# A fused attention and token-mixing block: its first operations written out engine by engine, phi loaded compact, x laid out by tiles

## The chip, the cores and the metric

One core of a Trainium2 chip runs the kernel. The metric is the device time of one execution in microseconds; lower is better. The engines are PE (TensorE, matrix products; its weight loads are listed as PEld), DVE (VectorE), ACT (ScalarE), POOL (GpSimd) and SP (SyncE, which issues most DMAs). Each runs its own list of instructions in order, and they wait for one another through semaphores.

## What is computed

x has 2048 rows (tokens) of 512 numbers. First an attention with a learned feature map, per head (32 heads of 16), then an MLP across the tokens:

```
xn  = layernorm(x)
q, k, v = split(xn @ wqkv)                                  # 32 heads of 16 each
phi(y)  = concat(softmax(y @ w_phi), softmax(-(y @ w_phi))) # per head
o   = phi(q) (phi(k)^T v) / (phi(q) (phi(k)^T 1) + 1e-6)
h   = x + o @ wo
y   = w2^T gelu(w1^T layernorm(layernorm(h)) + b1) + b2     # w1, w2 act on the token axis
out = h + y
```

Everything is in 32-bit floats. To keep the precision with the faster kind of product, the kernel splits each operand in a high part (a copy rounded by the operand type, `F32R`) and a low part (the difference), and takes three products: high·high, high·low and low·high.

## The kernel before

The tokens are cut into 16 tiles of 128 rows (`NT`), the 512 features into 4 blocks of 128 (`KD`). The kernel has three stages: attention with the K, V and Q projections (up to about 135 us of the span), then the attention's output and the first part of the MLP, then the two MLP products. The change touches the beginning of the first stage.

**Weights.** `wT` is the transposed `wqkv`, in 12 row blocks of 128 x 512: blocks 0 to 3 belong to Q, 4 to 7 to K, 8 to 11 to V. Each block c is loaded (`load_w`), freed of its mean (`center(c)`: the mean is taken off the weights so that the layernorm's mean need not be taken off x; even blocks on VectorE in three instructions, odd ones on ScalarE in two), brought to the orientation that the projections need (`fold(c)`, four matmuls: with the block-diagonal phi matrix `ph` for Q and K blocks, so that w_phi is folded into the weights, and as a plain transpose by `ident` for V blocks), and then split (`split_w`: the high part on ScalarE, the low part on VectorE). `fold` writes to a PSUM tile of `ps_q` or `ps_v`, with two buffers each.

**Tiles of x.** `load_x(t)` brings the transposed tile, `split_x(t)` splits it: the high part on ScalarE, the low part on GpSimd. `load_h(t)` brings the same rows untransposed, and `stats_x(t)` takes their variance: two ScalarE passes with accumulation, a small VectorE instruction and a power on GpSimd, which gives the scale `r1`.

**Projections.** `proj` is 12 matmuls of 512 columns: for each of 4 blocks the three products of `mm3`. `k_logits(t)` projects tile t on K and makes the logits with four VectorE instructions (`logit_ops`: a maximum, a minimum, two differences), then ScalarE takes the exponential (`exps`). `k_norm(t)` takes sums and reciprocals on VectorE and multiplies on GpSimd, which also adds up `zacc`. `v_proj(t)` projects on V, and ScalarE scales it with `r1`. `kv(t)` takes 32 small matmuls into one accumulator.

**Order.** The framework's planner sorts instructions of all engines by a model of their times. Inside a `manual_schedule` block the listed engines get the instructions of the block in the order of the program text; instructions from outside the block can still be placed between them. In the kernel before, the block at lines 267 to 301 lists VectorE and ScalarE, so the order of TensorE and GpSimd is the planner's. It covers the centering, folding and splitting of all weights, `split_x(0)`, `split_x(1)` and two `stats_x`. Then a loop over t = 0 to 14 (lines 330 to 349) has for each tile: the loads of tile t + 2, `k_logits(t)`, a `v_proj` except for t in `V_NOT` (5, 8 and 11), `kv` of a tile three back, `k_norm(t - 1)`, `split_x` and `stats_x` of t + 2, and, for t in `Q_AT`, one Q projection with its logits, exponential and sums. This loop is ordered by the planner on all engines. A later written block does the rest of V and goes on with Q.

**Buffers.** `xraw` has two buffers, `xh` three, `pk` six (`len(V_NOT) + 3`); `ps_k` and `ps_v` two each. `ps_k` also holds the target of nine warm-up matmuls that keep TensorE working while the first loads come in.

**Queue.** All loads go out on SP's queue, in the order of lines 215 to 233: two weight blocks, `ph` (256 KB, in rows of 512 bytes), two more weight blocks, `xraw` of tile 0, and so on. The transposed x is a matrix of 512 x 2048, so the rows of one tile's load are 512 bytes long.

Of the kernel before, what the change touches and what calls it, by code (L numbers as in the profile page):

```python
# [9 lines left out]
F32 = mybir.dt.float32  # L10
# [5 lines left out]
ET = mybir.EngineType  # L16

P = 128
# [6 lines left out]
Q_AT = (3, 5, 8, 9, 11, 13)  # L25
V_NOT = (5, 8, 11)
SUMS = 8
# [5 lines left out]
@with_exitstack  # L33
def block_kernel(ctx: ExitStack, tc: tile.TileContext, x, xT, wT, phibd, wo, w1, b1, w2, b2,
                 kvmask, ident_in, out):
# [60 lines left out]
    def load_x(t):  # L96
        raw = kk.tile([P, KD, P], F32, name="xraw")
        nc.sync.dma_start(raw, xT[:, t * P:(t + 1) * P].rearrange("(k p) s -> p k s", p=P))
        return raw
# [65 lines left out]
    def heads(e):  # L165
        return e.rearrange("p g (a d) -> p (g a) d", d=DH)

    def k_logits(t):
        PK[t] = kk.tile([P, NG, P], F32, name="pk", bufs=len(V_NOT) + 3)
        run(logit_ops(proj(t, wkh, wkl, ps_k, "pk_ps"), PK[t], False))  # L170
        exps(t, PK[t])
# [32 lines left out]

    with tc.tile_pool(name="prep", bufs=1) as prep:
        ph = prep.tile([P, 4, P], F32, name="ph")
        WR = {}
# [29 lines left out]

        def center(c):

            mu = prep.tile([P, 1], F32, name="mu", bufs=3)  # L240
            if c % 2 == 0:
                nc.vector.reduce_sum(mu, WR[c], axis=AX.X)
                nc.vector.tensor_scalar_mul(mu, mu, -1.0 / D)
                nc.vector.tensor_scalar(WR[c], WR[c], mu, None, op0=ALU.add)
            else:
                junk = prep.tile([P, D], F32, name="junk")
                nc.scalar.activation(junk, WR[c], AF.Copy, scale=-1.0 / D, accum_out=mu)
                nc.scalar.activation(WR[c], WR[c], AF.Identity, bias=mu)
# [9 lines left out]

        def split_w(c):
            hi, lo = HL[c // 4]  # L260
            cols = slice((c % 4) * P, (c % 4 + 1) * P)
            split(hi[:, :, cols], lo[:, :, cols], FO[c], nc.vector)

        warm = ps_k.tile([P, P], F32, name="pk_ps", tag="pk_ps")
        for _ in range(WARM):
            nc.tensor.matmul(warm, ones, ones, start=True, stop=True)
        with tc.manual_schedule(engines={ET.DVE, ET.Activation}):
            center(4)
            center(5)
            fold(4, ps_q, "pu")  # L270
            center(6)
            fold(5, ps_q, "pu")
            center(7)
            split_w(4)
            split_w(5)
            split_x(0, xr[0])
            fold(6, ps_v, "pv")
            split_w(6)
            fold(7, ps_v, "pv")
            split_w(7)  # L280
            center(8)
            center(9)
            fold(8, ps_q, "pu")
            fold(9, ps_q, "pu")
            center(10)
            center(11)
            split_w(8)
            split_w(9)
            fold(10, ps_q, "pu")
            fold(11, ps_q, "pu")  # L290
            split_x(1, xr[1])
            split_w(10)
            split_w(11)
            stats_x(0)
            stats_x(1)
            for c in range(4):
                center(c)
            for c in range(4):
                fold(c, ps_q, "pu")
                split_w(c)  # L300

# [446 lines left out]
def _layout(A_x, A_wqkv, A_w_phi, A_wo, B_w1, B_b1, B_w2, B_b2):  # L748
    x = np.asarray(A_x)[0]
    wqkv = np.asarray(A_wqkv)  # L750
    phi = np.asarray(A_w_phi)
    bd = np.zeros((4, P, P), np.float32)
    for h in range(H):
        b, o = divmod(h, P // DH)
        bd[b, o * DH:(o + 1) * DH, o * DH:(o + 1) * DH] = phi[h]
    mask = np.zeros((P, 64), np.float32)
    for a in range(P // DH):
# [6 lines left out]
        "x": x,  # L764
        "xT": x.T,
        "wT": wqkv.T,
        "phibd": bd,
        "wo": wo,
# [25 lines left out]
```

## Time and profile before

| | us |
|---|---|
| median of three timed runs | 545.8 (544.52, 545.8, 545.85) |
| the profiled execution's own time | 544.96 |
| its span | 543.2 |
| TensorE busy | 528.6 (97% of the span) |
| VectorE busy | 393.8 (73%) |
| ScalarE busy | 256.5 (47%) |
| GpSimd busy | 234.2 (43%) |

The span runs from the first to the last instruction of the execution that the profiler recorded; the time of an execution holds 1.76 us more here. A row of a timeline gives the start in us from the span's start, the duration, the engine, the line of the kernel, the operation, what is written and what is read, the shape, and in brackets how long the engine had been idle and what ended that. A row of the chain of waits gives start, length, engine, tile, line and count. In a row of grouped instructions the numbers after the bar are the busy time in us and the mean ns of one, then the idle time ahead of them. Matmuls are pipelined: one is listed with its latency, while the next one starts before it ends, so the cost of a matmul in a dense row is the distance of two starts.

### The profile page before, as it was taken

The page shows a single profiled execution, that of the slowest core. Times are in us where ns is not written, and L with a number is a line of the kernel's source. Part 1 is how long each engine was busy: PE and PEld are TensorE (multiplying, and loading weights), DVE is VectorE, ACT ScalarE, POOL GpSimd, SP SyncE. Part 2 cuts the span into 40 slices and gives each one's busy share as a digit, 9 for nine tenths or more (in the row PEclk, how much of TensorE's full clock was granted, in tenths as well). Part 3 has the DMA queues.
Part 4 walks back from the last instruction along what each step waited for, and adds up shares of the span by engine and source line. Part 5 has one row for each costly group of instructions (what it writes and reads, how often), then busy time and mean ns, then how long its engine had stood idle before and what let it go on. Part 6 is the DMA issues. An engine that isn't in the chain of part 4 may idle for free.

```text
span 543.2 us, 9896 instructions
## 1 busy us (share of the span) xinstructions
PE 528.6 (97%) x3872; PEld 449.7 (83%) x3872; DVE 393.8 (73%) x726; ACT 256.5 (47%) x402; POOL 234.2 (43%) x183
## 2 busy tenths in 40 slices
PE   7999999999999999999999999999999999999996
PEld 6687787877777777777787788888899999999996
DVE  4783999975689998996546862223947878878874
ACT  6599935334344555445546533224643433433330
POOL 1369799798978888997342200000001011101110
PEclk9999999999999999999999999999999999999998
DMA  8434402004121223333234543333103655535631
GB/s 307 128 117 118 134 22 58 2 1 138 38 60 59 81 76 117 118 117 118 98 118 154 173 140 97 97 97 97 39 14 107 152 138 134 136 133 121 156 73 45
DMA packets 52014, 56.06 MB, mean 103 GB/s; under 512 B 3840, under 2 KB 41600, under 8 KB 51968
## 3 DMA queue, kind: packets, MB, share of 16 engines
q1 hardware_dynamic: 49808, 51.64, 30.2%
q0 software_dynamic: 2016, 3.67, 4.9%
q8 instruction: 30, 0.49, 0.4%
q14 instruction: 16, 0.13, 0.1%
q10 hardware_dynamic: 144, 0.13, 0.1%
HBM read 47.04 MB, written 8.39 MB: 102 GB/s over the span
## 4 chain that ended last, share of the span: by engine, by line
PE 87%; DVE 7%; ACT 3%; DMA 2%; issue 1%; SPq 0%; DVEq 0%; ACTq 0%
PE py L687 25%; PE pu L61 11%; PE pu L63 11%; PE pu L62 10%; PE pk_ps L61 3%; PE pk_ps L62 3%; PE pk_ps L63 3%; PE po L61 3%; PE pv L61 3%; PE pv L62 3%; PE pv L63 3%; PE po L62 2%; PE po L63 2%; PE tn L468 2%; PE kvp L194 2%; PE tn L486 1%
## 5 line engine op out<-in xcount | busy, mean ns | idle before, releaser
L57 DVE TENSOR_TENSOR wlo<-wraw,whi 128x512 fp32r<-128x512 f32 (+1 forms) x84 | 99.6, 1197 | 72.4 <-ACT whi L56 72.3
L56 ACT ACTIVATE whi<-wraw 128x512 fp32r<-128x512 f32 (+1 forms) x84 | 81.9, 986 | 128.9 <-PE py L687 73.8
L725 POOL DMA_DIRECT2D out<-ot x14 | 12.4, 998 | 205.0 <-DVE ot L723 205.0
L687 PE MATMUL py<-uf,whi 128*128 128x256 f32 x560 | 96.2, 283 | 0.0
L61 PE MATMUL pu<-hs,whi 128*128 128x512 f32 x224 | 87.6, 394 | 0.6 <-ACT eq L140 0.6
L63 PE MATMUL pu<-hs,wlo 128*128 128x512 f32 x224 | 86.4, 392 | 1.1 <-DVE wlo L57 1.1
L62 PE MATMUL pu<-hs,whi 128*128 128x512 f32 x224 | 87.3, 390 | 0.0
L687 PEld LDWEIGHTS py<-uf,whi 128*128 128x128 f32 x560 | 83.3, 192 | 0.0
L687 PE MATMUL py<-uf,wlo 128*128 128x256 f32 x280 | 69.9, 283 | 0.0
L63 PEld LDWEIGHTS pu<-hs,wlo 128*128 128x128 f32 x224 | 41.7, 188 | 11.2 <-DVE wlo L57 2.7
L61 PEld LDWEIGHTS pu<-hs,whi 128*128 128x128 f32 x224 | 42.1, 188 | 9.5 <-ACT eq L140 1.1
L687 PEld LDWEIGHTS py<-uf,wlo 128*128 128x128 f32 x280 | 49.7, 192 | 0.0
L62 PEld LDWEIGHTS pu<-hs,whi 128*128 128x128 f32 x224 | 42.1, 188 | 8.4
L470 ACT ACTIVATE pht<-tn 128x512 f32<-128x512 f32 x32 | 17.4, 596 | 50.5 <-PE tn L468 50.5
L376 POOL TENSOR_TENSOR ez<-eq,zB 128x1024 f32<-128x1024 f32 x16 | 38.3, 2399 | 0.7 <-ACT zB L430 0.7
L687 PE MATMUL py<-un,whi 128*128 128x256 f32 x224 | 38.4, 283 | 0.0
L182 POOL TENSOR_TENSOR pk<-pk,sk 128x1024 f32<-128x1024 f32 x16 | 31.1, 1941 | 9.3 <-ACT xs L56 3.0
L687 PEld LDWEIGHTS py<-un,whi 128*128 128x128 f32 x224 | 33.2, 192 | 0.1
L394 POOL TENSOR_TENSOR eq<-eq,w 128x1024 f32<-128x1024 f32 x16 | 31.0, 1940 | 4.4 <-DVE w L391 4.4
L186 POOL TENSOR_TENSOR zacc<-zacc,pk 128x1024 f32<-128x1024 f32 x13 | 31.2, 2403 | 0.5
L57 POOL TENSOR_TENSOR xs<-xraw,xs 128x512 fp32r<-128x512 f32 x16 | 20.5, 1290 | 24.2 <-ACT xs L56 24.2
L57 POOL TENSOR_TENSOR hs<-hn,hs 128x512 fp32r<-128x512 f32 x16 | 20.6, 1289 | 21.2 <-ACT hs L56 21.2
(152 smaller groups left out, 1152.8 us busy)
## 6 DMA issues: line engine op xcount, KB each, us to landing
wraw<-in_w SPq DMA_DIRECT2D x112, 256.0 KB, 2.9
xraw<-in_xT SPq DMA_DIRECT2D x16, 256.0 KB, 3.1
xh<-in_x SPq DMA_DIRECT2D x16, 256.0 KB, 2.7
h<-in_x SPq DMA_DIRECT2D x16, 256.0 KB, 2.9
out<-h SPq DMA_DIRECT2D x16, 256.0 KB, 2.3
out<-ot POOLq DMA_DIRECT2D x14, 256.0 KB, 4.7
wraw<-in_wT SPq DMA_DIRECT2D x12, 256.0 KB, 5.1
wo<-in_wo SPq DMA_DIRECT2D x4, 256.0 KB, 4.5
```

The costliest lines, as they stand in the source:

```text
L56: nc.scalar.activation(hi, src, AF.Copy)
L57: lo_engine.tensor_sub(lo, src, hi)
L61: nc.tensor.matmul(o, ah, bh, start=first, stop=False)
L62: nc.tensor.matmul(o, ah, bl, start=False, stop=False)
L63: nc.tensor.matmul(o, al, bh, start=False, stop=last)
L182: nc.gpsimd.tensor_mul(heads(PK[t]), heads(PK[t]), sk.unsqueeze(2).to_broadcast([P, 2 * H, DH]))
L186: nc.gpsimd.tensor_add(zacc, zacc, PK[t])
L376: nc.gpsimd.tensor_mul(EZ[t], EQ[t], zB)
L394: nc.gpsimd.tensor_mul(heads(EQ[t]), heads(EQ[t]), W[t].rearrange("p g c h -> p (g c h)").unsqueeze(2).to_broadcast([P, 2 * H, DH]))
L470: nc.scalar.activation(PHT[t][:, half * 4:half * 4 + 4, :], ptr[:, half], AF.Copy)
L687: nc.tensor.matmul(o, a[x], b[:, y], start=start and i == 0, stop=stop and i == 2, skip_group_check=True)
L725: nc.gpsimd.dma_start(out[(t + i) * P:(t + i + 1) * P, :], flat(ot[:, i]), accum_op=ALU.add)
```

## The change

The first operations of all four computing engines are put into one `manual_schedule` block, and their order is written out.

- **phi.** Instead of the block-diagonal matrix of 4 x 128 x 128 the kernel gets `phic`, 128 x 72: the 64 columns of w_phi and an 8-column mask. It is loaded on ScalarE's queue, and one GpSimd multiplication with two broadcast operands makes `ph` from it.
- **x.** `xT` is laid out by tiles, so that each partition reads one row of 2 KB. `xraw` gets three buffers.
- **Loads.** SP's order is: w4 to w7, x0, x1, ident, w8 to w11, x2, h0, h1, x3, w0 to w3, h2, x4, h3, then the small ones.
- **Splitting weights.** `split_w` becomes `hi_w` (ScalarE, or VectorE for blocks 4 and 5) and `lo_w` (VectorE). Block 10 is centered on ScalarE instead of VectorE.
- **Order.** K is projected for tiles 0, 1 and 2 before the first V projection, with the V blocks' transposes between K1 and K2; then V0, K3, the folds of blocks 0 and 1, and V1. K0 is taken by parts (`by_part`): all four high·high products, then low-x·high, then high·low. Logits, exponentials, statistics and `k_norm(0)`, `k_norm(1)` stand at written places.
- **Loop.** It now begins at t = 3, with K from t = 4 and V from tile 2 at t = 4; `V_NOT` is (0, 1, 8).

```diff
-V_NOT = (5, 8, 11)
+V_NOT = (0, 1, 8)
...
-        raw = kk.tile([P, KD, P], F32, name="xraw")
-        nc.sync.dma_start(raw, xT[:, t * P:(t + 1) * P].rearrange("(k p) s -> p k s", p=P))
+        raw = kk.tile([P, KD, P], F32, name="xraw", bufs=3)
+        nc.sync.dma_start(raw, xT[t])
...
-    def proj(t, wh, wl, pool, name):
+    def proj(t, wh, wl, pool, name, by_part=False):
         o = pool.tile([P, D], F32, name=name, tag=name)
+        if by_part:
+            for i, (a, w) in enumerate(((0, wh), (1, wh), (0, wl))):
+                for kt in range(KD):
+                    nc.tensor.matmul(o, X[t][:, a, kt, :], w[:, kt, :], start=i == 0 and kt == 0,
+                                     stop=i == 2 and kt == KD - 1)
+            return o
...
-        load_w(4)
-        load_w(5)
-        nc.sync.dma_start(ph, phibd.rearrange("c p f -> p c f"))
-        load_w(6)
-        load_w(7)
-        xr = {0: load_x(0)}
-        load_w(8)
+        nc.scalar.dma_start(pc, phic)
+        for c in range(4, 8):
+            load_w(c)
+        xr = {0: load_x(0), 1: load_x(1)}
         nc.sync.dma_start(ident, ident_in)
-        load_w(9)
+        for c in range(8, 12):
+            load_w(c)
+        xr[2] = load_x(2)
         load_h(0)
-        load_w(10)
-        load_w(11)
-        xr[1] = load_x(1)
         load_h(1)
+        xr[3] = load_x(3)
         for c in range(4):
             load_w(c)
+        load_h(2)
+        xr[4] = load_x(4)
+        load_h(3)
...
-        def center(c):
+        def center(c, vector):
...
-            if c % 2 == 0:
+            if vector:
...
-        def split_w(c):
-            hi, lo = HL[c // 4]
-            cols = slice((c % 4) * P, (c % 4 + 1) * P)
-            split(hi[:, :, cols], lo[:, :, cols], FO[c], nc.vector)
+        def parts(c):
+            return [w[:, :, c % 4 * P:(c % 4 + 1) * P] for w in HL[c // 4]]
+
+        def hi_w(c, vector=False):
+            if vector:
+                nc.vector.tensor_copy(parts(c)[0], FO[c])
+            else:
+                nc.scalar.activation(parts(c)[0], FO[c], AF.Copy)
+
+        def lo_w(c):
+            hi, lo = parts(c)
+            nc.vector.tensor_sub(lo, FO[c], hi)
...
-        with tc.manual_schedule(engines={ET.DVE, ET.Activation}):
+        with tc.manual_schedule(engines={ET.PE, ET.DVE, ET.Activation, ET.Pool}):
+
+            nc.gpsimd.tensor_mul(ph.rearrange("p c (a f) -> p c a f", f=DH),
+                                 pc[:, 0:64].rearrange("p (c f) -> p c f", f=DH).unsqueeze(2).to_broadcast([P, 4, 8, DH]),
+                                 pc[:, 64:72].unsqueeze(1).unsqueeze(3).to_broadcast([P, 4, 8, DH]))
+            center(4, True)
+            center(5, False)
             fold(4, ps_q, "pu")
+            center(6, True)
             fold(5, ps_q, "pu")
+            center(7, False)
+            fold(6, ps_v, "pv")
+            fold(7, ps_v, "pv")
+            hi_w(4, True)
+            hi_w(5, True)
+            hi_w(6)
             split_x(0, xr[0])
+            hi_w(7)
+            for c in range(4, 8):
+                lo_w(c)
             split_x(1, xr[1])
+            k0 = proj(0, wkh, wkl, ps_k, "pk_ps", True)
+            center(8, True)
+            for c in range(9, 12):
+                center(c, False)
+            k1 = proj(1, wkh, wkl, ps_k, "pk_ps")
+            for c in range(8, 12):
+                fold(c, *((ps_q, "pu"), (ps_v, "pv"))[c // 10])
+            k_ops(0, k0)
+            split_x(2, xr[2])
+            k_ops(1, k1)
             stats_x(0)
+            k2 = proj(2, wkh, wkl, ps_k, "pk_ps")
+            for c in range(8, 12):
+                hi_w(c)
+            for c in range(8, 12):
+                lo_w(c)
+            exps(0, PK[0])
+            split_x(3, xr[3])
+            k_ops(2, k2)
+            v_proj(0)
             stats_x(1)
+            exps(1, PK[1])
+            k_norm(0)
+            k3 = proj(3, wkh, wkl, ps_k, "pk_ps")
+            center(0, True)
+            center(1, False)
+            split_x(4, xr[4])
+            k_ops(3, k3)
+            stats_x(2)
+            exps(2, PK[2])
+            fold(0, ps_q, "pu")
+            fold(1, ps_q, "pu")
+            hi_w(0)
+            hi_w(1)
+            lo_w(0)
+            lo_w(1)
+            v_proj(1)
+            k_norm(1)
+            center(2, True)
+            center(3, False)
+        stats_x(3)
+        exps(3, PK[3])
+        for c in range(2, 4):
+            fold(c, ps_q, "pu")
+            hi_w(c)
+            lo_w(c)
...
-    v = 0
-    for t in range(NT - 1):
+    v = 2
+    load_h(4)
+    stats_x(4)
+    for t in range(3, NT - 1):
         if t + 2 < NT:
             raw = load_x(t + 2)
             load_h(t + 2)
-        k_logits(t)
-        if t not in V_NOT:
+        if t > 3:
+            k_logits(t)
+        if t > 3 and t not in V_NOT:
             v_proj(v)
...
-        "xT": x.T,
+        "xT": x.reshape(NT, P, KD, P).transpose(0, 3, 2, 1),
...
-        "phibd": bd,
+        "phic": phic,
```

`k_ops(t, o)` is the first half of the old `k_logits`: it allocates `PK[t]` and makes the logits from the projected tile o.

More of the change, by code (lines that the diff above doesn't have):

```diff
@@ L33, in block_kernel @@
 @with_exitstack
-def block_kernel(ctx: ExitStack, tc: tile.TileContext, x, xT, wT, phibd, wo, w1, b1, w2, b2,
+def block_kernel(ctx: ExitStack, tc: tile.TileContext, x, xT, wT, phic, wo, w1, b1, w2, b2,
                  kvmask, ident_in, out):
@@ L166, in heads, with k_ops @@
         return e.rearrange("p g (a d) -> p (g a) d", d=DH)
+    def k_ops(t, o):
+        PK[t] = kk.tile([P, NG, P], F32, name="pk", bufs=len(V_NOT) + 3)
+        run(logit_ops(o, PK[t], False))
     def k_logits(t):
-        PK[t] = kk.tile([P, NG, P], F32, name="pk", bufs=len(V_NOT) + 3)
-        run(logit_ops(proj(t, wkh, wkl, ps_k, "pk_ps"), PK[t], False))
+        k_ops(t, proj(t, wkh, wkl, ps_k, "pk_ps"))
         exps(t, PK[t])
@@ L205, in block_kernel @@
     with tc.tile_pool(name="prep", bufs=1) as prep:
+        pc = prep.tile([P, 72], F32, name="pc")
         ph = prep.tile([P, 4, P], F32, name="ph")
@@ L266, in block_kernel @@
             nc.tensor.matmul(warm, ones, ones, start=True, stop=True)
-        with tc.manual_schedule(engines={ET.DVE, ET.Activation}):
-            center(4)
-            center(5)
+        with tc.manual_schedule(engines={ET.PE, ET.DVE, ET.Activation, ET.Pool}):
[4 more added lines that the diff above has]
+            center(5, False)
@@ L270, in block_kernel @@
             fold(4, ps_q, "pu")
-            center(6)
+            center(6, True)
             fold(5, ps_q, "pu")
-            center(7)
-            split_w(4)
-            split_w(5)
-            split_x(0, xr[0])
[L277 to L287, printed above, removed]
@@ L288, in block_kernel @@
-            split_w(9)
-            fold(10, ps_q, "pu")
-            fold(11, ps_q, "pu")
-            split_x(1, xr[1])
-            split_w(10)
-            split_w(11)
-            stats_x(0)
-            stats_x(1)
[L296 to L300, printed above, removed]
+            center(7, False)
+            fold(6, ps_v, "pv")
+            fold(7, ps_v, "pv")
+            hi_w(4, True)
@@ L751, in _layout @@
     phi = np.asarray(A_w_phi)
[L752 to L755, printed above, removed]
+    phic = np.concatenate([phi.reshape(4, P, DH).transpose(1, 0, 2).reshape(P, 64),
+                           np.kron(np.eye(8), np.ones((DH, 1)))], axis=1).astype(np.float32)
     mask = np.zeros((P, 64), np.float32)
```

## The prediction

> **What bounds the kernel now.** I read the page first, then busy time by stretches, then TensorE's waits.
>
> ```profile
> span 543.2 us, 9896 instructions
> PE 528.6 (97%) x3872; PEld 449.7 (83%) x3872; DVE 393.8 (73%) x726; ACT 256.5 (47%) x402; POOL 234.2 (43%) x183
> PE 87%; DVE 7%; ACT 3%; DMA 2%; issue 1%; SPq 0%; DVEq 0%; ACTq 0%
> ```
>
> TensorE is busy for 97% of the span and carries 87% of the chain that ended last. An edit ahead of the loops can only win TensorE time that is empty now. Stretches (length, then PE, PEld, DVE, ACT, POOL busy, clock, DMA share, GB/s):
>
> ```profile
> 0.00:5.19 5.19, 3.80 (x18) 3.64 (x19) 1.50 (x5) 2.42 (x4) 0.20 (x4) 1.00 0.65 200
> 5.19:24.14 18.95, 15.40 (x84) 12.10 (x85) 12.66 (x24) 10.89 (x23) 4.26 (x4) 1.00 0.71 243
> 24.14:60.00 35.86, 35.86 (x254) 28.83 (x255) 25.44 (x52) 34.54 (x79) 28.33 (x26) 1.00 0.42 123
> 60.00:120.00 60.00, 60.00 (x463) 47.60 (x463) 56.37 (x91) 28.66 (x41) 53.18 (x32) 1.00 0.12 34
> ```
>
> From 24.14 to 120 us TensorE has no gap at all, so what is won before 24.14 is kept as a shift, if that density is kept. Before 5.19 it runs only the warm-up. Between them, 84 matmuls take 18.95 us; these waits stand there (total us, times, longest), and the rows of the timeline and of the chain behind them give the prices:
>
> ```profile
> PE pk_ps L61 <- ACT wkh L56: 1.3, 1, 1.3
> PE pk_ps L61 <- ACT xs L56: 1.3, 1, 1.3
> PE pk_ps L62 <- DVE wkl L57: 0.3, 1, 0.3
> PE pu L254 <- DMA ph<-in_phibd: 0.3, 1, 0.3
> ```
> ```profile
> 5.19 2.02 PE L254 MATMUL pu<-ph,wraw 128*128 128x128 f32 x16 [0.33 <-DMA ph<-in_phibd]
> 11.44 0.49 PE L61 MATMUL pk_ps<-wkh,xs 128*128 128x512 f32 x1 [1.31 <-ACT wkh L56]
> 24.14 0.74 PE L61 MATMUL pv<-wvh,xs 128*128 128x512 f32 x2
> 29.98 0.39 PE L61 MATMUL pk_ps<-wkh,xs 128*128 128x512 f32 x1
> 33.38 0.39 PE L61 MATMUL pk_ps<-wkh,xs 128*128 128x512 f32 x1
> ```
> ```profile
> 15.09 0.45 PE pu L257 x4
> 33.77 0.89 PE pu L254 x8
> 38.31 0.58 PE kvp L194 x32
> ```
>
> From 29.98 to 33.38 lie 15 starts, so one 512-column matmul costs 0.227 us and a projection of twelve 2.72. A fold with phi costs 0.89, a fold by transpose 0.45. The 84 are four of each and three K projections: 3.56 + 1.80 + 8.16 = 13.5 us of work in 18.95. **5.4 us is to be had there**, plus what the first fold can start earlier.
>
> **The change, part by part.** *Loads.* The phi matrix of 256 KB, third in SP's queue, goes; a compact one of 37 KB goes out on ScalarE's queue, w4 to w7 follow one another, and x comes in 2 KB rows instead of 512-byte ones.
>
> ```profile
> 3.39 0.69 DVE L242 TENSOR_REDUCE mu<-wraw 128x1 f32<-128x512 f32 x1 [2.37 <-DMA wraw<-in_wT]
> 4.30 0.49 DVE L244 TENSOR_SCALAR wraw<-wraw,mu 128x512 f32<-128x512 f32 x1
> 5.93 0.69 DVE L242 TENSOR_REDUCE mu<-wraw 128x1 f32<-128x512 f32 x1 [1.15 <-DMA wraw<-in_wT]
> ```
> ```profile
> 4.02 0.63 ACT L247 ACTIVATE junk<-wraw 128x512 f32<-128x512 f32 x1 [2.00 <-DMA wraw<-in_wT]
> 4.78 0.72 ACT L248 ACTIVATE wraw<-wraw,mu 128x512 f32<-128x512 f32 x1
> 7.44 0.63 ACT L247 ACTIVATE junk<-wraw 128x512 f32<-128x512 f32 x1 [1.95 <-DMA wraw<-in_wT]
> ```
> ```profile
> 0.74 0.85 SPq L213 DMA_DIRECT2D wraw<-in_wT  x2
> ```
> ```profile
> 5.60:6.70 1.10, 1.10 (x12) 1.10 (x11) 0.74 (x2) 0.00 (x0) 0.00 (x0) 1.00 0.91 299
> 9.00:13.50 4.50, 2.85 (x14) 2.17 (x15) 3.79 (x8) 4.44 (x10) 1.27 (x1) 1.00 1.07 394
> ```
>
> The sums start when their tile lands: w4 3.39, w5 4.02, w6 5.93, w7 7.44. Spaced like w4 and w5 (0.63), or at 256 KB by 299 GB/s (0.88), w6 lands at 4.65 to 4.9 and w7 at 5.3 to 5.8. I take the former, as all rows are then long ones; worst is no change.
>
> The Trainium skill, "DMA: Bandwidth & Descriptors", section Specifications, gives line rate from 512 bytes up, so by it longer rows bring nothing. The trace speaks against it: 299 GB/s with 512-byte rows in flight, 394 without most of them. By the rule only phi's missing 0.9 us would count, w7 would land at about 6.6, and the gain would be some 0.4 us smaller.
>
> *Phi on GpSimd.* No row shows this multiply. The nearest are a plain 128x512 subtract and a broadcast multiply of twice the size:
>
> ```profile
> L57 POOL TENSOR_TENSOR xs<-xraw,xs 128x512 fp32r<-128x512 f32 x6 | 7.7, 1289 | 21.5 <-ACT xs L56 21.5
> L182 POOL TENSOR_TENSOR pk<-pk,sk 128x1024 f32<-128x1024 f32 x3 | 5.8, 1937 | 3.6 <-ACT pk L163 2.4 <-ACT sqj L113 1.2
> ident<-in_ident SPq DMA_DIRECT2D x1, 64.0 KB, 4.9
> ```
>
> So 0.97 to 1.29 us. Its load goes out at about 0.74 into empty engines; w4 took 2.65 us so, ident 4.9 under load. I take 3.3 for the landing and 4.6 for the end, because it is a seventh of w4 in size and not behind anything: hidden by center 4 on VectorE, which ends at 4.30 + 0.49 = 4.79. The late bound is 0.74 + 4.9 + 1.29 = 6.9, two us behind that cover.
>
> The Trainium skill, "GPSIMD Engine Reference", section Key points, lets GpSimd contend with VectorE for SBUF while VectorE is in a two-port mode. Center 4 falls into just this time; held for its 0.49, phi would end at 5.1 and cost 0.3 us of the gain. No row of this trace shows it.
>
> *The first folds.* Fold 4 starts at 4.87 instead of 5.19. Center 6 (VectorE) ends at 6.2, center 7 (ScalarE, 1.48 from 4.02 to 4.78 + 0.72, here from 5.5) at 7.0. Four folds at 0.89 then run without a gap to 8.43. The copies and differences:
>
> ```profile
> 16.33 0.68 DVE L138 TENSOR_TENSOR pk<-pk_ps,mx 128x512 f32<-128x512 f32 x1
> 16.93 0.68 DVE L57 TENSOR_TENSOR wvl<-pu,wvh 128x512 fp32r<-128x512 f32 x1
> 17.53 0.68 DVE L143 TENSOR_TENSOR pk<-mn,pk_ps 128x512 f32<-128x512 f32 x1
> ```
> ```profile
> 8.83 1.06 ACT L56 ACTIVATE wkh<-pu 128x512 fp32r<-128x512 f32 x2
> ```
>
> VectorE's go 0.60 apart, ScalarE's 0.52. ScalarE does hi 6, x0, hi 7 from 7.6 to 9.3; VectorE hi 4, hi 5 and the four lo parts by 10.0 (two hi parts moved onto it cost 1.2, in its idle time). K0 starts at 9.35, 2.1 earlier. By parts, its four x-lo products want GpSimd's 1.29 after x0 (10.1; they come at 10.5) and its four lo-weight products lo 7 (10.0; they come at 11.4): no wait. K0 ends at 12.3, K1 at 15.0, the four transposes at 16.8 (ScalarE's three centers take it from 9.8 to 14.3), K2, with x2's difference done at 16.2, at 19.7. The same work ended at 24.14: **4.4 us ahead.** Of the three projections only these go ahead of v0; the loads x2 to x4 have many us, though x3 now waits in SP's queue for x0's buffer (10.1) and holds w0 to w3, which nobody wants before 26.
>
> *What is late next.* First v0: its second matmul wants lo 11 of all columns, and VectorE reaches this after K1's logits (15.2 + 2.4), then four times 0.60: 20.15. TensorE loses 0.45. Then fold 0, after K3, which ends at 25.65:
>
> ```profile
> L112 ACT ACTIVATE sqj<-xh 128x512 f32<-128x512 f32 x7 | 4.4, 625 | 0.1
> L113 ACT ACTIVATE sqj<-xh,st 128x512 f32<-128x512 f32 x6 | 4.3, 715 | 0.0
> L112 ACT ACTIVATION_READ_ACCUMULATOR sqj<-xh 128x1 f32 x7 | 1.3, 189 | 0.0
> L180 DVE TENSOR_REDUCE sk<-pk 128x64 f32<-128x1024 f32 x4 | 4.9, 1218 | 1.7 <-ACT pk L163 1.6
> L181 DVE RECIPROCAL sk<-sk 128x64 f32<-128x64 f32 x3 | 1.6, 545 | 0.0
> ```
>
> ScalarE's written order has v0's copy (from 23.1) ahead of tile 1's statistics (0.63 + 0.72 and two reads of 0.19: some 1.6, as they overlap a little): 25.3. VectorE's order has their small follow-up, then k_norm 0 (1.22 + 0.55), then center 0 (1.4): 28.6. Behind fold 0 stand fold 1 and v1. So 3.0 us are open on TensorE unless the planner puts free work there. It can: in the rows above, K0's logits (L138, L143), outside the written block, stand between written differences (L57) on an engine whose order was written already. The second v tile's projection, 2.72 us, has its inputs by then. I take it as filled, 0.3 left.
>
> Sum: 4.4 - 0.45 - 0.3 = **3.65 us** ahead, carried to the end. The profiled execution took 544.96 us (543.2 span, 1.76 around it): 541.3. The three timed runs have the median 545.8; those and the profiled one average 545.3, so I say **541.6**.
>
> Other edits are nothing: the other v order trades two projections between iterations; VectorE has 10.4 us idle from 24.14 to 60 to hide what shifts, and the same work falls due without that.
>
> **Rivals.**
> 1. *The written order is kept strictly and the 3.0 us stay.* For it: fold 0 is next in the list, and the planner's durations need not show it a gap. Against: the interleaving above. Gain 0.95: 544.3.
> 2. *The change doesn't do what it says: phi or w7 come late.* Against: short queue, fewer bytes. At the late bound of phi, two us go: 543.6.
> 3. *VectorE becomes the bound in the loop, and it is slower.* A K tile costs it 4 x 0.60 + 1.77 = 4.2, a Q tile 2.4 and two sums of half a tile (0.68 each, an estimate from the rows of that size above), 3.8: 8.0 against TensorE's 2 x 2.72 + 0.58 = 6.0 in an iteration with Q and no V. VectorE is at 56.37 of 60 us after 60. If the V tiles run ahead to fill the first gaps, three such iterations lack cover: 3 x 2.0 - 3.65 = 2.35 lost, 547.6. It decides when the 10.4 us of VectorE idle before 60 are used up. Against: only iterations 3 and 8 are now without V (before 5, 8 and 11), and VectorE starts its logits earlier too.
>
> **How the numbers follow.** Forecast 0.55 (540.2 to 543.0); strict order 0.14; late phi or loads 0.10; slower 0.16; more than 4.4 won, as waits I counted are filled too, 0.05. Differences below 0.3% (1.6 us) can't be told from none. Faster: 0.55 + 0.05 + half of late (0.05) = 0.65; same: 0.14 + 0.05 = 0.19; slower 0.16. The range reaches from a little under the gain of 5.4 to over the strict order: 539.4 to 545.4, leaving out the slower rival.
>
> **What would show it.** K0's first matmul near 9.4, v0's near 19.7, fold 4 near 4.9 (phi right); w7's sum on ScalarE near 5.5; a V matmul between K3 and fold 0 (filled) or a gap of about 3 us (strict); no gap between 30 and 120 us. Gaps there behind VectorE's logits would prove me wrong, as would a first fold at 6 us or later.

## The result and the profile after

The changed kernel is **slower**: 549.75 us (median of four executions, 549.49 to 550.26) against 545.16 (544.35 to 545.85) for the kernel before. The ratio is 1.0086, with a 95% interval from 1.0066 to 1.0106. The profiled execution took 550.26 us, its span 548.5.

The page's first rows, and busy time by the stretches used for the kernel before; the third runs up to the product of `zacc` by ones (line 483), the first work of the stage's end that needs `k_norm` of all tiles:

```profile
span 548.5 us, 9904 instructions
PE 531.9 (97%) x3872; PEld 452.5 (82%) x3872; DVE 396.6 (72%) x725; ACT 257.2 (47%) x403; POOL 235.5 (43%) x184
```
```profile
5.19:24.14 18.95, 18.08 (x98) 15.23 (x98) 16.61 (x29) 13.61 (x28) 5.68 (x5) 1.00 0.75 257
24.14:60.00 35.86, 32.15 (x229) 26.03 (x228) 18.57 (x37) 33.04 (x78) 25.62 (x23) 0.95 0.38 110
60.00:138.41 78.41, 76.58 (x618) 59.18 (x617) 71.22 (x111) 34.06 (x46) 65.17 (x38) 1.00 0.16 48
```

The beginning did what it was written for: 98 matmuls by 24.14 us against 84. Then TensorE, which had no gap from 24.14 to 120 us before, is busy for 32.15 of 35.86 us. VectorE, 25.44 us busy there before, is busy for 18.57, so it has more left: 71.22 us up to the `zacc` product. The last stretch of the kernel before, and the product in its timeline:

```profile
60.00:132.75 72.75, 72.42 (x603) 57.06 (x603) 65.70 (x103) 34.06 (x49) 63.73 (x37) 1.00 0.17 53
```
```profile
132.75 1.96 PE L429 MATMUL pk_ps<-zacc,ones 128*128 128x512 f32 x4 [0.33 <-DVE zacc L424]
```

TensorE's timeline of the changed kernel, and stretches of 1 us (the third number from the end is its clock):

```profile
1.06 4.21 PE L284 MATMUL pk_ps<-ones 128*128 128x128 f32 x18 [1.06 <-DVE mhalf L52]
5.23 2.82 PE L264 MATMUL pu<-ph,wraw 128*128 128x128 f32 x16
...
10.63 2.10 PE L123 MATMUL pk_ps<-wkh,xs 128*128 128x512 f32 x8 [0.80 <-ACT wkh L276]
...
20.88 0.47 PE L61 MATMUL pv<-wvh,xs 128*128 128x512 f32 x1
...
26.55 0.39 PE L63 MATMUL pk_ps<-wkh,xs 128*128 128x512 f32 x1
30.65 3.68 PE L264 MATMUL pu<-ph,wraw 128*128 128x128 f32 x16 [3.71 <-DVE wraw L254]
33.99 0.57 PE L61 MATMUL pv<-wvh,xs 128*128 128x512 f32 x1
...
50.41 1.95 PE L264 MATMUL pu<-ph,wraw 128*128 128x128 f32 x16
...
138.41 1.95 PE L483 MATMUL pk_ps<-zacc,ones 128*128 128x512 f32 x4 [1.83 <-DVE zacc L478]
```
```profile
30.00:31.00 1.00, 0.35 (x2) 0.35 (x3) 1.00 (x2) 1.00 (x4) 0.94 (x2) 0.89 0.00 0
31.00:32.00 1.00, 1.00 (x7) 1.00 (x7) 1.00 (x3) 1.00 (x3) 1.00 (x2) 0.50 0.00 0
32.00:33.00 1.00, 1.00 (x6) 1.00 (x6) 1.00 (x3) 0.94 (x5) 1.00 (x2) 0.50 0.00 0
33.00:34.00 1.00, 1.00 (x8) 1.00 (x6) 0.20 (x2) 0.97 (x3) 1.00 (x2) 0.50 0.62 178
34.00:35.00 1.00, 1.00 (x6) 0.88 (x6) 0.00 (x0) 0.97 (x3) 0.98 (x2) 0.90 0.62 139
```

The product comes 5.66 us later, and the span is 5.3 longer: the whole loss lies ahead of it. No V matmul stands between K3 and fold 0: TensorE waits there for 3.71 us, and the granted clock is 0.50 from 30.7 to 34.2 us, so that folds 0 and 1 take 3.34 us from start to the next start instead of twice 0.89. VectorE's timeline, and GpSimd's:

```profile
26.43 0.15 DVE L115 TENSOR_SCALAR ve<-st 128x1 f32<-128x1 f32 x1 [2.71 <-ACT sqj L113]
26.50 1.21 DVE L189 TENSOR_REDUCE sk<-pk 128x64 f32<-128x1024 f32 x1
...
28.22 0.63 DVE L252 TENSOR_REDUCE mu<-wraw 128x1 f32<-128x512 f32 x1
...
29.07 1.52 DVE L254 TENSOR_SCALAR wraw<-wraw,mu 128x512 f32<-128x512 f32 x1
...
38.49 1.29 DVE L280 TENSOR_TENSOR wql<-pu,wqh 128x512 fp32r<-128x512 f32 x2 [1.30 <-ACT wqh L276]
39.69 2.33 DVE L189 TENSOR_REDUCE sk<-pk 128x64 f32<-128x1024 f32 x2
...
43.60 1.19 DVE L254 TENSOR_SCALAR wraw<-wraw,mu 128x512 f32<-128x512 f32 x1
...
58.44 0.69 DVE L151 TENSOR_REDUCE mx<-pu 128x32 f32<-128x512 f32 x1 [2.11 <-PE pu L63]
59.04 0.68 DVE L152 TENSOR_REDUCE mn<-pu 128x32 f32<-128x512 f32 x1
59.64 0.68 DVE L151 TENSOR_REDUCE mx<-pk_ps 128x32 f32<-128x512 f32 x1
```
```profile
3.75 1.05 POOL L287 TENSOR_TENSOR ph<-pc 128x512 f32<-128x512 f32 x1 [3.30 <-DMA pc<-in_phic]
...
28.38 1.93 POOL L191 TENSOR_TENSOR pk<-pk,sk 128x1024 f32<-128x1024 f32 x1 [1.16 <-DVE sk L190]
```

Q0's logits (`pu`, 58.44) stand ahead of K4's (`pk_ps`, 59.64) in VectorE's list. K4 was projected by 43 us, but Q0 needs all of Q's weights, and these were late. ScalarE's rows show where they were held:

```profile
30.20 0.61 ACT L112 ACTIVATE sqj<-xh 128x512 f32<-128x512 f32 x1
...
36.84 1.14 ACT L169 ACTIVATE pk<-pk,r 128x1024 f32<-128x1024 f32 x1
37.88 1.06 ACT L276 ACTIVATE wqh<-pu 128x512 fp32r<-128x512 f32 x2
```

Folds 0 and 1 had ended at 34, but their high parts (line 276) are written behind the exponential of tile 2 (36.84), with the statistics of four tiles ahead of that from 30.20, three of them from outside the block, set there by the planner. Until the parts are taken, both buffers of `ps_q` are full, and no further fold and no Q0 has a place to go; and VectorE's list goes on as written: the low parts (38.49), `k_norm(1)` (39.69), and only then center 2 (done at 44.8). Folds 2 and 3 run at 50.41, behind V matmuls.

### The profile page after: what moved, and what is told of

The parts are those of the page before. It is cut to its first block, busy times and chain, and to the rows that moved or that the text cites. A ratio compares the mean times of both kernels' runs of the same rounds, so it can differ in the third digit from the quotient of the medians.

```text
span 548.5 us, 9904 instructions
## 1 busy us (share of the span) xinstructions
PE 531.9 (97%) x3872; PEld 452.5 (82%) x3872; DVE 396.6 (72%) x725; ACT 257.2 (47%) x403; POOL 235.5 (43%) x184
## 4 chain that ended last, share of the span: by engine, by line
PE 84%; DVE 9%; ACT 3%; issue 2%; DMA 1%; POOL 1%; SPq 0%; DVEq 0%; POOLq 0%; ACTq 0%
PE py L741 25%; PE pu L61 10%; PE pu L63 10%; PE pu L62 10%; PE po L61 3%; PE pv L61 3%; PE pv L62 2%; PE pk_ps L61 2%; PE pv L63 2%; PE pk_ps L63 2%; PE po L62 2%; PE pk_ps L62 2%; PE po L63 2%; PE tn L522 2%; PE kvp L203 2%
## 5 line engine op out<-in xcount | busy, mean ns | idle before, releaser
L448 POOL TENSOR_TENSOR eq<-eq,w 128x1024 f32<-128x1024 f32 x16 | 31.0, 1937 | 4.4 <-DVE w L445 4.4
L61 PE MATMUL po<-woh,oh 128*128 128x512 f32 x64 | 26.6, 416 | 1.0 <-DVE h L564 1.0
```

Source lines behind the costliest of these rows:

```text
L61: nc.tensor.matmul(o, ah, bh, start=first, stop=False)
L448: nc.gpsimd.tensor_mul(heads(EQ[t]), heads(EQ[t]), W[t].rearrange("p g c h -> p (g c h)").unsqueeze(2).to_broadcast([P, 2 * H, DH]))
```

## The experiments

Each was timed beside the kernel before on the same chip; ratios are to that. The columns in the middle are readings like those above: VectorE's busy time from 24.14 to 60 us, what it still does from 60 us to the `zacc` product, that product's start, and TensorE's wait for it. They are read from one execution of each run, the profiled one; in e1, e2, e7 and e11 this one took 1.0, 2.6, 1.8 and 2.7 us longer than the run's median; in the others the two differ by less than 0.9 us. Runs that were timed on different chips are compared by what each differs from the kernel before beside it.

| run | median us (runs) | ratio, 95% interval | VectorE 24-60 | left | `zacc` at | wait |
|---|---|---|---|---|---|---|
| before | 545.16 (4) | 1 | 25.44 | 65.70 | 132.75 | 0.33 |
| changed | 549.75 (4) | 1.0086 [1.0066, 1.0106] | 18.57 | 71.22 | 138.41 | 1.83 |
| e1 | 547.52 (4) | 1.0062 [1.0047, 1.0077] | 20.50 | 67.43 | 133.76 | 3.54 |
| e2 | 546.99 (4) | 1.0046 [1.0029, 1.0062] | 21.56 | 67.74 | 134.97 | 3.52 |
| e3 | 552.12 (4) | 1.0141 [1.0123, 1.0158] | 17.33 | 72.31 | 139.01 | 4.11 |
| e4 | 548.42 (4) | 1.0076 [1.0061, 1.0091] | 22.21 | 67.36 | 134.55 | 3.53 |
| e5 | 542.54 (10) | 0.9964 [0.9949, 0.9978] | 25.43 | 60.84 | 130.49 | 0.33 |
| e6 | 550.17 (4) | 1.0102 [1.0071, 1.0132] | 23.78 | 65.84 | 137.85 | 1.43 |
| e7 | 543.15 (10) | 0.9975 [0.9958, 0.9992] | 24.99 | 66.42 | 133.58 | 0.34 |
| e8 | 544.21 (10) | 0.9987 [0.997, 1.0005] | 28.10 | 63.09 | 132.09 | 0.28 |
| e9 | 548.71 (4) | 1.0059 [1.0036, 1.0083] | 23.35 | 64.51 | 133.78 | 3.93 |
| e10 | 539.81 (4) | 0.9901 [0.9885, 0.9917] | 27.15 | 59.45 | 128.36 | 0.28 |
| e11 | 546.14 (10) | 1.0031 [1.0011, 1.005] | 21.36 | 66.62 | 133.95 | 2.84 |
| e12 | 541.32 (4) | 0.9935 [0.9917, 0.9954] | 28.84 | 60.52 | 129.47 | 0.28 |
| e13 | 546.9 (10) | 1.0036 [1.0019, 1.0053] | 21.40 | 65.93 | 133.27 | 2.84 |
| e14 | 545.0 (10) | 0.9997 [0.998, 1.0013] | 22.93 | 64.32 | 133.62 | 0.33 |
| e15 | 539.87 (4) | 0.9907 [0.9884, 0.9931] | 25.39 | 59.99 | 128.35 | none |
| e16 | 541.34 (4) | 0.9935 [0.9915, 0.9955] | 27.32 | 62.44 | 129.75 | none |
| e17 | 542.96 (10) | 0.9966 [0.9949, 0.9983] | 23.81 | 65.00 | 131.19 | 0.95 |
| e18 | 539.55 (4) | 0.9903 [0.9869, 0.9937] | 29.30 | 57.35 | 128.16 | none |

### The gap: e1 to e4

e1 has centers 0 and 1 earlier:

```diff
             k_ops(2, k2)
+            center(0, True)
+            center(1, False)
...
-            center(0, True)
-            center(1, False)
             split_x(4, xr[4])
```

> The centering of the Q blocks 0 and 1 is moved up in the written order, to right behind tile 2's logits, so that neither stands behind tile 1's statistics. Theory A (the loss is the gap of 3.7 us between K3 and fold 0, and the half clock that follows it, 1.6 us): both vanish, K3, folds and V1 run on without a gap at full clock, about 549.75 - 5.3 = 544.4 us. Theory B (the loss comes from the loop, by the new order of V and VectorE that falls behind; the gap only moves it): the gap vanishes but reappears in the loop or before the zacc product, 548 us or more.

e2 writes V1 ahead of the folds:

```diff
+            v_proj(1)
             fold(0, ps_q, "pu")
...
-            v_proj(1)
```

> V1 is written ahead of folds 0 and 1; everything else stays. Theory A: V1 covers 2.7 of the 3.9 us between K3 and fold 0, some 1.2 us stay open, too short for the clock to fall, so 549.75 - 2.7 - 1.6 = 545.5 us. Theory B: 548 us or more.

e3 keeps TensorE working in the gap; the products are overwritten by the fold:

```diff
-        def fold(c, pool, name):
+        def fold(c, pool, name, busy=0):
             FO[c] = pool.tile([P, KD, P], F32, name=name, tag=name)
+            for _ in range(busy):
+                nc.tensor.matmul(FO[c][:, 0, :], ones, ones, start=True, stop=True)
...
-            fold(0, ps_q, "pu")
+            fold(0, ps_q, "pu", 14)
```

> 14 products of ones are added in front of fold 0; they write into the fold's own tile and are overwritten, so the wait for center 0 stays as it is but TensorE is busy in it (14 x 0.22 = 3.1 us). If the half clock of the two folds comes from the idle time, they take 1.8 us again instead of 3.3 and the time is 549.75 - 1.5 = 548.2 us. If it comes from something else, 549.75 us.

e4 takes V1 out of the written block and leaves its place to the planner:

```diff
-            v_proj(1)
...
+        v_proj(1)
         stats_x(3)
```

> V1 is taken out of the written order and left to the planner; the rest stays written. The planner then puts V1, V2 and K4 ahead of fold 0. Theory A: no gap beyond a few tenths, full clock, about 544.5 us; it also says that the written place of V1 is what kept the planner from filling. Theory B: 548 us or more.

**Measured.** The gap goes in e1, e2 and e4. In e4 the planner itself sets V matmuls ahead of fold 0, the last of them here:

```profile
31.25 0.39 PE L63 MATMUL pv<-wvh,xs 128*128 128x512 f32 x1
31.48 1.95 PE L264 MATMUL pu<-ph,wraw 128*128 128x128 f32 x16
```

So it can fill that place, and what kept it from doing so in the changed kernel was V1, written *behind* the folds. In e3 the folds run at full clock, 1.81 us to the next start:

```profile
27.00 3.29 PE L263 MATMUL pu<-ones 128*128 128x128 f32 x28
30.87 2.05 PE L266 MATMUL pu<-ph,wraw 128*128 128x128 f32 x16 [0.58 <-DVE wraw L254]
32.68 0.47 PE L61 MATMUL pv<-wvh,xs 128*128 128x512 f32 x1
```

The half clock thus comes from the idle time ahead of it. But the times moved far less than expected, or, in e3, the other way: TensorE gets to the `zacc` product earlier and waits there, 3.5 to 4.1 us, with a half clock behind. From this product to the end of the span these four take 411.6 to 413.0 us, the kernel before 410.5 and the changed one 410.1: with a product 0.6 us later, that is how e3 got slower though its folds were faster. e1:

```profile
129.56 0.65 PE L203 MATMUL kvp<-pk,vs 128*32 128x64 f32 x32
133.76 3.75 PE L483 MATMUL pk_ps<-zacc,ones 128*128 128x512 f32 x4 [3.54 <-DVE zacc L478]
136.52 1.42 PE L61 MATMUL pu<-wqh,xs 128*128 128x512 f32 x1
```

**What follows.** Filling the gap moves the wait. VectorE is late at the stage's end whether or not TensorE idles at 27 us: its work left at 60 us is 67 to 72 us in these four, against 65.7 in the kernel before.

### Q later, Q earlier, and the parts alone: e5 to e12

e5 centers all four Q blocks early, moves the statistics and the exponential of tile 2 behind the splits of blocks 0 and 1, and writes the folds and splits of blocks 2 and 3 into the block (its whole tail; the loop over c = 2 and 3 behind the block goes):

```diff
             k_ops(2, k2)
+            center(0, True)
+            center(1, False)
+            center(2, True)
+            center(3, False)
...
             k_ops(3, k3)
-            stats_x(2)
-            exps(2, PK[2])
             fold(0, ps_q, "pu")
             fold(1, ps_q, "pu")
...
             lo_w(1)
+            stats_x(2)
+            exps(2, PK[2])
             v_proj(1)
             k_norm(1)
-            center(2, True)
-            center(3, False)
+            fold(2, ps_q, "pu")
+            fold(3, ps_q, "pu")
+            hi_w(2)
+            hi_w(3)
+            lo_w(2)
+            lo_w(3)
```

> All four Q blocks are centered right behind tile 2's logits, in the 2.7 and 3.0 us in which VectorE and ScalarE waited, and their folds and splits follow in the written block. Theory C (in VectorE's list the logits of Q0 stand ahead of those of K4, so VectorE starves until the last Q block is split; from Q0's logits to the zacc product lay 79.0 to 80.1 us in all six kernels so far): Q0's logits start near 40 us instead of 58.4, VectorE is no longer the bound, the product of zacc comes when TensorE has done its work, near 130 us instead of 138.4, and the time is 541 to 542.5 us. Theory D (the last K tiles are simply placed late by the planner, whatever Q0 does): the product still waits 3 us or more for zacc and the time stays at 545 to 547.5 us.

e6 is the changed kernel with its first two Q tiles later in the loop:

```diff
-Q_AT = (3, 5, 8, 9, 11, 13)
+Q_AT = (5, 6, 8, 9, 11, 13)
```

> The changed kernel with the first two Q projections in iterations 5 and 6 instead of 3 and 5; nothing else. Theory C: the logits of K4 and K5 are no longer behind Q0's in VectorE's list, come near 45 us instead of 59.6, fill its idle time, and the product of zacc comes 3 to 5 us earlier: 545 to 547 us, although the gap of 3.7 us on TensorE stays. Theory A (the gap and the half clock are the loss): no change, 549.75 us.

e7 is the kernel before with phi made on GpSimd and x laid out by tiles, the old loads, block and loop kept:

```diff
-        nc.sync.dma_start(ph, phibd.rearrange("c p f -> p c f"))
+        nc.scalar.dma_start(pc, phic)
...
+        nc.gpsimd.tensor_mul(ph, ...)
...
-        nc.sync.dma_start(raw, xT[:, t * P:(t + 1) * P].rearrange("(k p) s -> p k s", p=P))
+        nc.sync.dma_start(raw, xT[t])
```

> The kernel before with only the compact phi, spread out on GpSimd, and x by tiles; its order and loop stay. K0 starts up to 1 us earlier. Theory C: what decides is when Q0's logits start, and that hangs on ScalarE's and VectorE's lists between 24 and 53 us, not on the first loads: within 1.5 us of before. Theory E (the early part is worth what it wins on TensorE): 1 us faster.

e8 is the kernel before with e6's `Q_AT`; e9 and e10 are e1 and e5 with it; e11 is e1 with centers 2 and 3 also behind `k_ops(2, k2)`; e12 is e7 with e6's `Q_AT`.

> The kernel before with the first two Q projections in iterations 5 and 6; nothing else. In it TensorE is without a gap from 24 to 132 us and the product of zacc waits only 0.3 us, so the lists of VectorE and TensorE end together: theory C expects no gain beyond 0.5 us, 544 to 545 us, as TensorE is the bound as soon as VectorE has slack.

> The kernel of the early centers (e1) and, as well, the first two Q projections in iterations 5 and 6. e1 closed the gap on TensorE and then waited 3.5 us for zacc. Theory C (VectorE became the bound there because the logits of K4 and K5 stood behind those of Q0): with K4 and K5 ahead the wait for zacc falls below 1 us, no half clock follows it, and the time is 542.5 to 544.5 us. Theory D (the last K tiles are placed late whatever Q0 does): the wait stays at 3 us or more and the time at 547 us.

> The kernel with all Q blocks early (e5) and, as well, the first two Q projections in iterations 5 and 6. In e5 VectorE is busy for only 52.9 of the 60 us after 60 and TensorE has no gap from 24 to 130 us, so theory C expects no further gain: 542.5 us within 0.8 us. If VectorE were still the bound, 540 to 541 us.

> The kernel of the early centers (e1) with blocks 2 and 3 centered there as well; their folds stay outside the written block. Theory F (Q's blocks 2 and 3 are ready too late; until Q0's logits VectorE starves and TensorE has only V tiles to run, so all 12 V tiles of the loop are spent before K14's logits and none covers the wait for zacc): folds 2 and 3 come before 42 us instead of 48.4, Q0's logits before 50 instead of 54.8, fewer than 12 V tiles are done by K14's logits, the wait for zacc is below 1 us, and the time is 541.5 to 543.5 us. Theory G (the planner's order of the last tiles comes out as it will; only the written folds of e5 helped): 12 V tiles, a wait of 3 us or more, 547 us.

> The kernel before with compact phi and x by tiles (e7) and with the first two Q projections in iterations 5 and 6 (e8); no written order beyond the one it had. If the two small gains (1.4 and 0.4 us) add, 542.5 to 543 us; if the written order is what the 5 us of e10 need, no better than that.

**Measured.** e5 is the first that beats the kernel before, by 2.0 us. Q later wins nothing on the changed kernel and on e1 (e6, e9): in e6 VectorE has 5.4 us less left at 60 us than in the changed kernel, but idles 4.8 us more behind that (137.85 - 60 - 65.84 = 12.0 against 7.2). On top of e5 it wins 3.5 us (e10: 5.5 below the kernel before, e5 2.0), which was not expected. The layout alone is worth 1.4 us (e7); with Q later it is 3.4 (e12), more than e7's 1.4 and e8's 0.4 together (e8's interval holds 1). e11 has the centers early, and its profiled execution still a wait of 2.84 us.

**What follows.** The centers are not enough; something else in e5 made Q's weights early: its written folds, or the place of tile 2's exponential.

### Which edit made Q's weights early: e13 to e18

e13 writes folds 2 and 3 into e11's block; e14 and e15 are the changed kernel and e1 with Q's weight blocks 2 and 3 split from the folded blocks 0 and 1 (their own centers and folds are left out); e16 is the kernel before with the same left out.

```diff
             lo_w(0)
             lo_w(1)
+            for c in range(2, 4):
+                FO[c] = FO[c - 2]
+                hi_w(c)
+                lo_w(c)
...
-            center(2, True)
-            center(3, False)
...
-        for c in range(2, 4):
-            fold(c, ps_q, "pu")
-            hi_w(c)
-            lo_w(c)
```

> e11 with the folds and splits of Q blocks 2 and 3 written behind k_norm(1), and nothing else moved (in e5 the statistics and exponential of tile 2 were moved too). Theory G (VectorE is the bound from 60 us on; how much work it still has there is set by when Q's weights are ready, because Q0's logits stand ahead of K4's in its list): VectorE's busy time between 24.14 and 60 goes from e11's 21.4 us to about 25, what it has left up to the zacc product from 66.6 to about 61 to 63, TensorE's wait for zacc from 2.8 to 0.3, time 542 to 543.5. Theory H (it was the move of tile 2's statistics that e5 won by): as e11, 546 within 1, VectorE's work left over 65.

> The changed kernel, in which Q's weight blocks 2 and 3 are split from the folded blocks 0 and 1, so that their own centering and folding (0.9 us of TensorE, 1.3 of VectorE, 1.5 of ScalarE) are left out; VectorE's list has Q0's logits ahead of K4's as before. The gap of 3.7 us ahead of fold 0 and the half clock behind it stay. Theory G: Q0's logits come some 8 us or more earlier than 58.4, VectorE's busy time from 24.14 to 60 rises from 18.6 to 23 or more, its work left at 60 falls from 71.2 to 66 or less, and the kernel takes 545 to 546.5. Theory J (the loss behind the gap comes from the planner's order or the V tiles that run ahead, whatever Q's weights do): only the work left out is won, 548.5 to 549.2, and VectorE has 69 or more left.

> e1 (centers 0 and 1 early, so no gap) with the same work left out as in e14_after_half. Theory G: VectorE's work left at 60 falls from 67.4 to 63 or less, TensorE's wait for zacc from 3.5 to under 1.5 without a half clock behind it, time 541 to 543. Theory J: 546 to 547, wait for zacc 3 or more.

> Control: the kernel before with the same work left out (Q blocks 2 and 3 split from folded blocks 0 and 1). Its Q weights were ready in time (last fold 42.4, Q0's logits 53.6), so both theories expect little more than the 0.9 us of TensorE: 543 to 544.7. If it wins 3 us or more, what e14 and e15 win isn't the changed kernel's own loss.

e17 moves two lines of e1, and e18 the same two of e11:

```diff
             k_ops(3, k3)
-            stats_x(2)
-            exps(2, PK[2])
             fold(0, ps_q, "pu")
...
             lo_w(1)
+            stats_x(2)
+            exps(2, PK[2])
             v_proj(1)
```

> e1 with the statistics and the exponential of tile 2 written behind the splits of Q blocks 0 and 1 instead of ahead of the folds. In e1 and e13 ScalarE's list holds the high parts of blocks 0 and 1 behind that exponential (35.89 in e13, 28.08 in e5, although fold 1 had ended at 27.8), and both buffers of the folds and of Q's projections stay taken till then. Theory H (this place on ScalarE is what makes Q's weights late): last fold from 48.4 to 44 or earlier, VectorE's work left at 60 from 67.4 to 65 or less, 545 to 546.5, not less, since blocks 2 and 3 are still centered last. Theory J (it is the planner's order, whatever Q's weights do): 547.5 within 0.8.

> e11 (all four centers early) with the same move; folds 2 and 3 are left to the planner. Theory H: together these two moves are all that e5 won by: last fold near 34 to 38, Q0's logits at 48 to 50, VectorE's work left at 60 about 61 to 62.5, wait for zacc 0.3, time 542 to 543.5. If written folds are needed as well: 544.5 to 546.5 with a last fold after 42.

**Measured.** e13 is no better than e11: written folds do nothing while the buffers are taken. e17 wins 5.0 us on e1 by two lines (from 3.1 above the kernel before to 2.0 below), more than expected; e18 wins 6.9 on e11, more than expected too, and is, with e10, the best that does the whole work, 5.4 us below the kernel before. ScalarE in e1, where folds 0 and 1 had begun at 26.70, and in e17 (rows of the exponentials and of the high parts):

```profile
35.41 1.14 ACT L169 ACTIVATE pk<-pk,r 128x1024 f32<-128x1024 f32 x1
36.46 1.06 ACT L276 ACTIVATE wqh<-pu 128x512 fp32r<-128x512 f32 x2
```
```profile
29.13 1.06 ACT L276 ACTIVATE wqh<-pu 128x512 fp32r<-128x512 f32 x2
...
36.36 1.14 ACT L169 ACTIVATE pk<-pk,r 128x1024 f32<-128x1024 f32 x1
```

Q0's logits on VectorE, in e1 and in e17:

```profile
54.82 0.69 DVE L151 TENSOR_REDUCE mx<-pu 128x32 f32<-128x512 f32 x1 [2.65 <-PE pu L63]
```
```profile
52.35 0.69 DVE L151 TENSOR_REDUCE mx<-pu 128x32 f32<-128x512 f32 x1 [0.98 <-PE pu L63]
```

They come 2.5 us earlier in e17, and the `zacc` product 2.6 (133.76 to 131.19); the other 2.7 us between the two spans (546.8 and 541.5) lie behind the product, where e1's half clock is missing. In e11 and e13 the date of Q0's logits does not tell as much: they come at 53.66 and 52.98, but the product at 133.95 and 133.27, hardly other than in e1. And VectorE (third busy column) in e1 and in e18:

```profile
24.14:60.00 35.86, 35.63 (x290) 29.32 (x289) 20.50 (x43) 30.23 (x70) 26.91 (x24) 1.00 0.33 114
60.00:133.76 73.76, 70.22 (x557) 54.10 (x556) 67.43 (x105) 35.54 (x49) 63.74 (x37) 0.99 0.14 48
```
```profile
24.14:60.00 35.86, 35.86 (x258) 29.02 (x257) 29.30 (x54) 32.17 (x69) 29.66 (x25) 1.00 0.39 114
60.00:128.16 68.16, 68.16 (x587) 53.90 (x586) 57.35 (x92) 31.41 (x48) 60.66 (x36) 1.00 0.16 51
```

In e18 TensorE has no gap from 24.14 up to the product. The control e16 missed: leaving that work out wins 3.5 us on the kernel before too, not 0.9; its Q0's logits come at 48.44 instead of 53.56, so Q's weights were not early in the kernel before either. e14 and e15 are therefore read against e16, as if the work left out were worth the same 3.5 us in them, which no run shows. The four kernels then make a table of two causes (us against their own control):

| | Q blocks 2, 3 as written | split from blocks 0, 1 |
|---|---|---|
| gap of 3.7 us | +4.6 (changed) | +3.7 (e14 - e16) |
| no gap | +3.1 (e1) | -1.5 (e15 - e16) |

**What follows.** Two causes cover each other. Taking one away wins 0.9 or 1.5 us; taking both away wins 6.1, and then the early part's lead shows as a gain. e17, 2.0 us below the kernel before, says the same with the whole computation in place. Not tried: the move of the two lines without e1's centers, and the statistics or the exponential alone.

## Why the prediction was wrong

**Right, or off by little.** The loads: ScalarE began center 7 at 5.91 (5.5 said). Phi: 3.75 + 1.05 = 4.80 on GpSimd (4.6 said, 0.97 to 1.29 for the multiply), ahead of fold 4, which begins where the warm-up ends (5.23 for 4.87). V0 comes at 20.88 for 19.7: **3.3 us ahead of before's 24.14, not 4.4.** Of the missing 1.1 us, 0.4 is fold 4's start and 0.8 the first folds, which take 2.82 us for 16 where before took 2.02. e2 and e6, whose text is the same up to there, took 2.02, so it varies by execution; in all kernels with this beginning V0 starts between 20.12 (e5) and 21.16 (e3), and in some fold 7 waits for center 7 as well (0.57 us in e2). Why the first folds vary is open: the granted clock of that stretch reads 1.00. A rule of the Trainium skill, "TensorE: Matmul & The Clock Gate", section Part 1, would fit: the number of cold matmuls at a start varies from run to run, as the clock's window runs freely.

**Failed: "I take it as filled, 0.3 left."** The open stretch was found, its size nearly right (3.0 said, 3.71 measured), and so was the chain ahead of it. The argument for its filling was that the planner had set free work between written instructions before. It does, but not past a written V1: e4 shows it filled as soon as V1 is free. Rival 1 had the right event. Two prices of it were missing. Center 0's last instruction took 1.52 us instead of 0.49 beside GpSimd's multiplication (shown further down); and the folds behind the gap ran at half clock, 1.56 us (3.34 - 1.78; e3 shows 1.81 without idle time).

**Failed: "VectorE has 10.4 us idle from 24.14 to 60 to hide what shifts, and the same work falls due without that."** With the gap closed (e1) the kernel still lost 3.1 us. VectorE's idle time in that stretch did not shrink but grew to 17.3 us (35.86 - 18.57). Rival 3 named the result, VectorE as the bound of the loop's end, but looked for its cause in the loop's own work per tile. The cause lies in the written block. The prediction followed the queue behind fold 0 on TensorE, not the one behind `exps(2, PK[2])` on ScalarE, where `hi_w(0)` and `hi_w(1)` stand. Behind those stand the low parts, `k_norm(1)`, center 2, the folds 2 and 3, Q0, and behind Q0's logits K4's. That the place of `exps(2, PK[2])` and its statistics costs the time is shown by e17, 5.0 us for two lines, and e18; that all of it runs through Q0's logits is argued from the rows, and e13 speaks against "all": it has them only 0.6 us behind e17's, but VectorE 2.4 us less done by 60 us (21.40 against 23.81).

**Failed: "carried to the end".** A lead is kept only if all that the stage's end needs is early. TensorE's lead was handed to the wait for `zacc` in e1 to e4, and the half clock behind that wait took more.

Open: why Q later wins on top of e5 and e7 but not of the changed kernel and e1, and why leaving out half of Q's folding is worth 3.5 us to the kernel before; every such edit also reorders the loop.

## What to carry to other kernels

Where an order is written out, check for each engine what stands behind an instruction that waits: here an exponential on ScalarE held two PSUM buffers and a chain of steps on three engines, and the price fell due 100 us later. This planner filled a gap only with work that wasn't itself written behind it. A lead won at the start counts at the first point where all engines meet; before pricing it, add up what the second busiest engine still has to do up to there.

## What the runs showed of the hardware

TensorE's clock after an idle stretch: in or behind each wait of 3.5 to 4.1 us (at fold 0 in the changed kernel, e6 and e14; at the `zacc` product in e1, e2, e3, e4 and e9) it was granted 0.50; after 1.83 us (changed kernel at 138.41) it stayed at 1.00.

Read in slices of 0.1 us, the low stretch lasted either 3.4 us (changed, e2, e3, e4, e6) or twice that, 6.8 (e1, e9, e14). The length of the wait alone does not decide: e11 and e13 waited 2.84 us each and then had 6.8 and 3.4 us of it, and e7's profiled execution had 3.4 from 11.6 us, with no wait over 1.31 ahead of it. Of the ten executions of e11, five took 545.0 to 545.9 us at a mean granted clock of 0.998 and three 548.6 to 548.8 at 0.993, with two between; that fits a low stretch that comes or stays away in the same program, but only one of them has a trace.

The Trainium skill, "TensorE: Matmul & The Clock Gate", section Part 1, puts the drop at one idle window of some 3.4 us; the traces agree but for those of e7, e11 and e13. e1 at the `zacc` product:

```profile
134.00:135.00 1.00, 1.00 (x2) 0.48 (x3) 0.00 (x0) 0.00 (x0) 1.00 (x2) 0.50 0.06 16
135.00:136.00 1.00, 1.00 (x2) 0.42 (x2) 0.00 (x0) 0.16 (x1) 0.75 (x1) 0.50 0.00 0
136.00:137.00 1.00, 1.00 (x3) 0.34 (x1) 0.00 (x0) 0.44 (x1) 0.00 (x0) 0.50 0.00 0
```

VectorE's addition of the negative mean (line 254), 0.49 us before, took 1.52 beside GpSimd's multiplication from 28.38, whose own 1.93 us are what it took before (1937 ns), and 0.65 for center 4 beside the multiplication that makes phi, where the prediction had looked for the price on phi's side. In e5, where GpSimd idles from 21.9 to 25.9, it took 0.48:

```profile
23.79 0.48 DVE L254 TENSOR_SCALAR wraw<-wraw,mu 128x512 f32<-128x512 f32 x1
```

The Trainium skill, "GPSIMD Engine Reference", section 1. Specifications, has the two engines share their SBUF interfaces, with contention when VectorE's instruction is in a two-port mode or has two SBUF inputs. No row shows the mode of this one; the rows show that VectorE was the one held.
